# Zero products put into the finished order, and a start in which TensorE transposes the first tiles

## The chip, the cores and the metric

The kernel runs on one core of a Trainium2 chip. The core has five engines that run side by side, each with its own queue of instructions: TensorE (PE in the profile, with PEld for its weight loads), VectorE (DVE), ScalarE (ACT), GpSimd (POOL) and SyncE (SP), which here issues all DMAs. [...] TensorE writes into eight banks of PSUM, each of 128 partitions by 512 numbers of 32 bits; operands lie in SBUF.

The metric is the device time of one execution in microseconds (us), lower is better. The profile comes from one execution on the chip.

## The reference

Four residual layers work on one sequence x of 2048 tokens by 512 features in bf16: attention, a feed-forward block, then both again with the same weights.

```
x = x + attention(layernorm(x), wqkv, wo)      # 32 heads of 16 features, all 2048 keys for each query
x = x + ffn(layernorm(x), w1, b1, w2, b2)      # 512 -> 1376 -> 512, tanh form of gelu
x = x + attention(layernorm(x), wqkv, wo)
x = x + ffn(layernorm(x), w1, b1, w2, b2)

attention: q, k, v = split(y @ wqkv);  p = softmax(q k' / 4);  out = concat(p v) @ wo
ffn:       gelu(y @ w1 + b1) @ w2 + b2
```

The layernorm has no scale or shift. In the softmax one exp is taken for every head, query and key: 32 x 2048 x 2048 of them in each of the two attention layers.

## The kernel before

The text of the kernel is a planner. `Builder` holds generators, one for each piece of work, that hand tasks to `Sched`. `Sched.run` keeps a model of when each engine is free and when each operand is ready (`Prog.op`, `Prog.ready`), and picks again and again the task that can start first, by priority where several can. Each instruction carries a planned duration, written in the code; from them come the order of the instructions on each engine and which of them share work. After the last task, `finalize` puts in the semaphore waits, and the program is issued engine by engine. On the chip only the order and the waits are left; the planned times have no force there.

**Tiling.** Tokens are handled in 16 tiles of 128. A segment is one group of four heads (hg, 8 of them) with one chunk of 512 queries. The first chunk of layer 1 is done in two parts: keys 0 to 511 first, so that scores can start when four token tiles are through, then the other 1536 keys. Layer 3 splits its first chunk in the same way (1536 keys, then 512), and its last 512 queries into two units of 256.

**Scores.** A score tile is 128 keys by 512 queries of one head (L1240, a matmul on 32 rows of the array, four heads side by side). Most tiles go to ScalarE, which takes the exp of two banks at a time at the start, and of three and two in turn once six banks are free ("wide"), into the tile PT (L1225). Other tiles go to DVE: L1317 forms a bit pattern that stands for the exp, in two tiles of a pair, and L1348 makes three shifted copies of the pair; POOL scales values for them (L1101). Which tiles go to DVE is decided while the order is made, in `take_d`, by how late DVE is in the plan. L1409 multiplies the weights with V into one bank, ACCB, on 32 columns of the array per head.

**Other stages.** `job_first_tile` takes token tiles 0 to 3 of layer 1: layernorm (L808 to L821), a transpose by DMA into yT (L968), K, Q and V matmuls (L989), copies to SBUF (L1000, L1012, L1027), sums of squares for a bound on the scores (L941). Queries go to q_scr in DRAM (L1020) and come back transposed as qraw (L1074), from which L1086 makes QT. `job_qkv_tile` does the same for all other tiles (matmuls L876). `job_post` does the output projection, layernorm and the feed-forward block of a chunk, `job_tail` that of the last unit. SP issues the DMAs in the planned order, each in turn.

**Zero products.** `fill_pe` is called by `Sched.run` whenever TensorE would have a gap of more than 0.2 us in the plan. It looks at how busy the array was in the last 3.41 us of the plan, and where that is under 0.62 it puts matmuls with zero weights into the gap (L1150 on four column tiles, L1153 on the whole array). They add nothing to a result; they are part of the plan like other work, so what is planned later starts behind them. In the lines that follow, `need` is how many are wanted and `n` how many are put in.

```
n = int((gap - (PE_SWITCH if P.tiling == "col" else 2 * PE_SWITCH if P.tiling == "row" else PE_SWITCH) + FILL_OVER) / FILL_T)
need = int((FILL_ACT - P.activity(end)) * 3.41 / FILL_T + 0.999)
n = min(n, need, 80)
```

## Time and profile before

| what | value |
|---|---|
| time, median of 6 runs | 1642.71 us (1640.72 to 1645.58) |
| the profiled execution | 1642.72 us, of which the span from first to last instruction is 1640.9 us |
| granted clock of TensorE, mean over the span | 0.996 |
| ACT busy | 1562.0 us, 95% |
| PE busy | 1554.8 us, 95% |
| DVE busy | 1481.2 us, 90% |
| POOL busy | 379.4 us, 23% |
| exps on ScalarE (L1225) | 1304 instructions, 1485.8 us |
| score tiles on DVE (L1317) | 869 instructions, 584.4 us |
| zero products (L1150) | 2928 instructions, 143.0 us |

Busy time is the time in which an engine has at least one instruction in work; matmuls overlap, so their mean durations are longer than the steps between them. A group of instructions is shown as line, engine, operation, what it writes and reads with shapes, count, then busy us and mean ns, then the engine's idle time just before such instructions and who ended most of it. A row of windows gives, for one stretch of the span, its length and the busy time of PE, PEld, DVE, ACT and POOL with counts, then the clock that TensorE was granted, the mean share in which the DMA engines were busy, and GB/s. A row of the order of time gives start, length, engine, line, operation and count, and in brackets the idle time ahead of it with what ended it.

### The profile page before, as it was taken

Reading aid. Unit: us, or ns where it says so; the run is one execution under the profiler, and the core shown is the slowest. Engines: PE = TensorE matmul, PEld = TensorE weight load, DVE = VectorE, ACT = ScalarE, POOL = GpSimd, SP = SyncE. Lnnn points to the kernel's source line nnn. Section 1 sums busy time; section 2 is a strip of 40 time slices with the busy share of each in tenths; the row PEclk is TensorE's granted clock in tenths of the full one; section 3 lists DMA queues with packets and bytes.
Section 4 is the critical chain, followed back from the end, with each engine's and each line's share of the span. In section 5 each row is a group of like instructions: output and inputs, shape, how many; then the busy total and the mean of one; then the engine's idle time right before and its main releaser. Section 6 shows DMA issues by size and latency. Waiting matters only on the chain.

```text
span 1640.9 us, 40475 instructions
## 1 busy us (share of the span) xinstructions
PE 1554.8 (95%) x16682; PEld 504.1 (31%) x16833; DVE 1481.2 (90%) x3255; ACT 1562.0 (95%) x1383; POOL 379.4 (23%) x575
## 2 busy tenths in 40 slices
PE   8989999999999999999999998999999999999998
PEld 4222222222222222222232222322222222344444
DVE  7789999989999899989979799999899989999894
ACT  4989999999999999999999999899999999999996
POOL 4354332111320112111121134511011101222220
PEclk9999999999999999999999999999999999999999
DMA  6572000103111121112291330000000100010000
GB/s 174 103 138 56 21 8 8 43 17 65 63 24 36 32 44 57 33 30 46 86 127 45 64 84 15 18 21 8 14 11 8 21 12 8 6 19 10 23 8 14
DMA packets 181238, 66.34 MB, mean 40 GB/s; under 512 B 160859, under 2 KB 175424, under 8 KB 181056
## 3 DMA queue, kind: packets, MB, share of 16 engines
q1 hardware_dynamic: 181056, 63.75, 17.6%
q8 instruction: 135, 2.21, 0.5%
q14 instruction: 47, 0.39, 0.1%
HBM read 19.96 MB, written 15.30 MB: 21 GB/s over the span
## 4 chain that ended last, share of the span: by engine, by line
PE 48%; DVE 26%; ACT 21%; issue 3%; DMA 1%; POOL 1%; DVEq 0%; SPq 0%
ACT PT L1225 20%; PE ps L1240 19%; PE ps L1409 14%; DVE dp L1317 9%; DVE dp L1348 7%; PE ps L1574 4%; PE ps L1536 4%; PE ps L1503 3%; PE ps L876 3%; PE ps L1150 2%; DVE accT L1439 1%; ACT h L1566 1%; DVE n L941 1%; DVE OT L1479 1%; DVE QT L1086 1%
## 5 line engine op out<-in xcount | busy, mean ns | idle before, releaser
L1225 ACT ACTIVATE PT<-ps 128x1024 bf16<-128x1024 f32 (+1 forms) x1304 | 1485.8, 1251 | 49.1 <-PE ps L1240 42.7
L1240 PE MATMUL ps<-QT,KT 32*128 32x512 bf16 (+1 forms) x4608 | 685.4, 358 | 44.7 <-DVE dp L1317 15.5
L1317 DVE TENSOR_SCALAR dp<-ps 128x512 uint16<-128x512 f32 x869 | 584.4, 680 | 76.2 <-PE ps L1240 72.1
L1348 DVE TENSOR_SCALAR dp<-dp 128x1024 uint16<-128x1024 uint16 (+1 forms) x1323 | 515.7, 431 | 7.0 <-PE ps L1409 1.9
L1409 PE MATMUL ps<-PT,V 128*17 128x512 bf16 (+1 forms) x3624 | 487.8, 359 | 0.5 <-DVE accT L1439 0.4
L1101 POOL TENSOR_SCALAR vs<-V 128x340 bf16<-128x340 bf16 (+3 forms) x240 | 242.8, 1012 | 846.5 <-PE ps L1409 809.2
L1409 PE MATMUL ps<-dp,vs 128*17 128x512 bf16 (+1 forms) x2952 | 434.4, 356 | 1.2 <-DVE dp L1348 0.9
L1240 PEld LDWEIGHTS ps<-QT,KT 32*128 32x128 bf16 x4608 | 178.0, 91 | 575.5 <-issue 152.5
L1409 PE MATMUL ps<-dp,V 128*17 128x512 bf16 (+1 forms) x984 | 208.6, 358 | 1.5 <-DVE accT L1439 0.6
L1409 PEld LDWEIGHTS ps<-PT,V 128*17 128x17 bf16 x3624 | 116.0, 88 | 114.8 <-issue 103.2
L1409 PEld LDWEIGHTS ps<-dp,vs 128*17 128x17 bf16 x2952 | 109.5, 88 | 126.5 <-issue 107.0
L1150 PE MATMUL ps<-wqkv,zw 128*32 128x256 bf16 x2928 | 143.0, 278 | 0.6 <-DVE accT L1439 0.6
L1536 PE MATMUL ps<-yT,wf 128*128 128x512 bf16 (+3 forms) x356 | 93.7, 357 | 6.9 <-issue 4.3
L876 PE MATMUL ps<-wqkv,xnT 128*128 128x512 bf16 x299 | 85.4, 387 | 9.2 <-issue 2.9
L1150 PEld LDWEIGHTS ps<-wqkv,zw 128*32 128x32 bf16 x2928 | 73.4, 96 | 59.0 <-issue 41.8
L1439 DVE STREAM_TRANSPOSE accT<-ps 128x512 f32<-128x512 f32 (+1 forms) x88 | 57.9, 658 | 10.4 <-PE ps L1409 10.2
L1503 PE MATMUL ps<-wo,OT 128*128 128x512 bf16 x209 | 60.8, 382 | 5.0 <-issue 3.7
L1560 DVE TENSOR_SCALAR h<-ps,b1c 128x512 bf16<-128x512 f32 (+2 forms) x88 | 61.8, 702 | 3.9 <-PE ps L1536 3.5
L1409 PEld LDWEIGHTS ps<-dp,V 128*17 128x17 bf16 x984 | 51.1, 88 | 45.5 <-issue 24.9
L1479 DVE STREAM_TRANSPOSE OT<-ob 128x512 bf16<-128x512 bf16 (+1 forms) x72 | 45.9, 638 | 0.2
L1536 PEld LDWEIGHTS ps<-yT,wf 128*128 128x128 bf16 (+1 forms) x396 | 27.7, 99 | 53.1 <-issue 29.7
L1574 PE MATMUL ps<-wf,h 128*128 128x512 bf16 x143 | 40.8, 382 | 3.1 <-issue 1.7
(171 smaller groups left out, 774.6 us busy)
## 6 DMA issues: line engine op xcount, KB each, us to landing
wf<-in_B_w_dram SPq DMA_DIRECT2D x90, 128.0 KB, 2.3
q_scr<-qk SPq DMA_DIRECT2D x22, 256.0 KB, 2.1
k_scr<-qk SPq DMA_DIRECT2D x12, 256.0 KB, 2.0
out_dram<-xres SPq DMA_DIRECT2D x16, 128.0 KB, 1.7
v_scr<-vst SPq DMA_DIRECT2D x12, 136.0 KB, 1.9
V<-v_scr SPq DMA_DIRECT2D x8, 204.0 KB, 4.9
wqkv<-in_A_wqkv_dram SPq DMA_DIRECT2D x3, 512.0 KB, 5.7
q_scr<-h SPq DMA_DIRECT2D x6, 256.0 KB, 2.0
```

Of the source, the lines that this page charges most:

```text
L876: yield Task("pe", prio, [I(lambda e, c=c: e.matmul(self.ps[:, b, :], lhsT=xnT[:, c, :], rhs=self.wqkv[:, c, which * 512:which * 512 + 512 ...
L1101: yield Task("pool", 0.8, [I(lambda e, k=k: e.tensor_scalar(out=self.vs[:, q, k - 1, i:i + n, :], in0=src, scalar1=WSHIFT[k], scalar2=None ...
L1150: P.op("pe", lambda e, p=p: e.matmul(self.ps[p:p + 32, b, 0:w], lhsT=self.zw[:, 0:32], rhs=rhs[:, 0:w], start=st, stop=st, skip_group_chec ...
L1225: S_.submit(Task("act", 1e-5 * gi, [I(lambda e, pt=pt, n=n, b0=b0: e.activation(out=self.PT[:, pt:pt + n, :], in_=self.ps[:, b0:b0 + n, :] ...
L1240: return [I(lambda e, kb=kb, i=i: e.matmul(self.ps[:, b, i * W:(i + 1) * W], lhsT=self.KT[32 * hp:32 * hp + 32, hg, kb * 128:(kb + 1) * 12 ...
L1317: self.S_.submit(Task("dve", 0.0, [I(lambda e: e.tensor_scalar(out=self.dp[:, u, w * 512:(w + 1) * 512], in0=self.ps[:, b, :], scalar1=BIT ...
L1348: yield Task("dve", pr, [I(lambda e, k=k, v=v: e.tensor_scalar(out=self.dp[:, v, 0:N], in0=self.dp[:, u, 0:N], scalar1=float(SHIFT[k]), sc ...
L1409: ops.append((i, I(lambda e, hp=hp, v=v, ap=ap[:, i * W:(i + 1) * W], first=first and i == 0, W=W: e.matmul(self.ps[32 * hp:32 * hp + 17, ...
L1439: yield Task("dve", 0.3, [I(lambda e: e.transpose(self.accT[:, a, 0:W], self.ps[:, ACCB, 0:W]), [("ps", ACCB)], [RA], 0.17 + 0.535 * W / 5 ...
L1503: yield Task("pe", pr, [I(lambda e, hg=hg, i=i, b=b: e.matmul(self.ps[:, b, :], lhsT=self.OT[:, hg, i * 128:(i + 1) * 128], rhs=self.wo[:, ...
L1536: yield Task("pe", pr, [I(lambda e, c=c: e.matmul(self.ps[0:M, b, off:off + W], lhsT=self.w1(fc, c), rhs=self.yT[:, c, 0:W], start=(c == 0 ...
L1574: yield Task("pe", pr, [I(lambda e, fc=fc, i=i, b=b: e.matmul(self.ps[:, b, :], lhsT=self.gt(fc, i, W), rhs=self.w2(L, fc), start=(fc == 0 ...
```

## The change

Line numbers of the diff's new side are not those of the profile.

**Zero products.** `fill_pe` no longer puts any in while the order is made; it still lets DVE take a score tile in a long gap. When the order is finished, `refill` walks through it once more with a fresh model: before each TensorE instruction it computes the gap that the plan leaves, and puts in passes of four zero matmuls of 256 columns as long as the least busy stretch of 3.414 us around that moment holds less than 0.45 of the array. The order of all other instructions stays as it was made. A pass may go to ACCB, to the spare bank, or to a score bank whose contents have been read. Zero matmuls read `zw` alone, now 256 columns wide.

**Start.** All of x for tiles 0 to 3 is loaded ahead of the three weight slices. The other x tiles come in six pieces of two tiles, from a task of their own (`late`): it starts after the K store of tile 3, and the last four pieces wait for the query load of segment 2. Before, there were two pieces of four and eight tiles. `job_first_tile` transposes the normalised tile with four TensorE transposes and a copy by ScalarE in place of the DMA. The constants on DVE that aren't needed at once become tasks of priority 1.9.

**Planned durations and small rules.** DMA durations are set anew, and a DMA with a size also waits for a model of the shared bus; exps go from 0.174 + 0.428 n to 0.19 + 0.4275 n for n banks, the overlap of ScalarE's instructions from 0.127 to 0.128, the shifted copies of L1348 from 0.151 to 0.163 plus the same slope; PV_IDLE, the time after which a small batch of L1409 is let go, from 0.25 to 0.5; the post work of chunk 2 in layer 1 gets priority 0.95 in place of 1.6; batches of L1409 are sorted by turn.

The built programs differ in these counts: exps of three, two and one banks 620, 683, 1 before and 617, 682, 0 after; score tiles on DVE 869 and 881; pairs of shifted copies 1284 and 1305, single ones 39 and 33; zero matmuls of 32 columns of weights 2928 (256 wide) and 136 (128 wide) before, and 3216 (256 wide) after; zero matmuls on the whole array 154 (128 wide) and 36 (256 wide) before, none after; four yT transposes by DMA before, sixteen on TensorE and four copies on ScalarE after.

```diff
@@ Prog.op
         op.t0 = max(self.free[eng], self.ready(eng, reads, writes, same_ok))
         if eng == "sp":
             self.free[eng] = op.t0 + dur
-            op.t1 = op.t0 + dur + (2.0 if lat is None else lat)
+            lat, size = lat if isinstance(lat, tuple) else (2.0 if lat is None else lat, 0.0)
+            op.t1 = max(op.t0 + dur + lat, self.bus + 0.9)
+            if size:
+                self.bus = max(self.bus, op.t1 - size) + size
+                op.t1 = self.bus
@@ build_startup
         ldx(0, 1)
-        ldw(1, 512)
         ldx(1, 2)
         ldx(2, 4)
+        ldw(1, 512)
         ldw(0, 0)
         ldw(2, 1024)
-        self.S_.when([("ks", 1, 1)], lambda: ldx(4, 8))
-        self.S_.when([("ks", 1, 3)], lambda: ldx(8, 16))
+        def late():
+            yield ("keys", [("ks", 1, 3)])
+            for a in range(4, 16, 2):
+                if a == 8:
+                    yield ("keys", [("qraw", 2)])
+                yield self.dma(lambda e, a=a: e.dma_start(self.xres[:, a:a + 2, :], xr[:, a:a + 2, :]), [], [("x", a), ("x", a + 1)], 1.7, 0.5, (2.24, 1.04))
+                self.S_.mark(("xld", a))
+        self.S_.spawn(late(), 1.7)
@@ job_first_tile
-        yield self.dma(lambda e: e.dma_start_transpose(xnT, xnr), [RX], [RXT], prio, 1.25)
+        b = yield ("get", "mb")
+        yield Task("pe", prio - 0.5, [I(lambda e, k=k: e.transpose(self.psbf(b)[:, k * 128:(k + 1) * 128], xnr[:, k * 128:(k + 1) * 128], self.ident[:, :]), ...) for k in range(4)])
+        yield Task("act", prio - 0.5, [I(lambda e: e.activation(out=xnT, in_=self.psbf(b)[:, 0:512].rearrange("p (c t) -> p c t", c=4), func=ACTF.Copy), ...)])
+        S_.release("mb", b)
@@ fill_pe, refill
-        n = min(n, need, 80)
...
+        def need(t):
+            k = int(t / FILL_DT)
+            lo = max(0, k - m + 1)
+            s = sum(act[lo:lo + m])
+            best = s
+            for j in range(lo, min(k, n - m - 1)):
+                s += act[j + m] - act[j]
+                best = min(best, s)
+            return FILL_U * FILL_W - best
...
+            t0, b, st = min(banks)
+            d = FILL_N / 2400.0
+            while t0 + d <= end and need(t0 + d / 2) > 0.0:
+                for p in range(4):
+                    z = self.zero(b, p, FILL_N, st)
+                    P.op("pe", z[0], z[1], z[2], z[3], z[4], z[5])
+                add(t0, t0 + d, 1.0)
+                t0 += d
+        for op in old.ops:
+            if op.eng == "pe":
+                fill(op)
+            P.op(*op.spec)
@@ flow_scores
-                                                [("ps", b) for b in banks], [("pt", pt + k) for k in range(n)], 0.174 + 0.428 * n)]),
+                                                [("ps", b) for b in banks], [("pt", pt + k) for k in range(n)], 0.19 + 0.4275 * n)]),
@@ try_pv
-PV_IDLE = 0.25
+PV_IDLE = 0.5
@@ post_prio
-        return 0.95 if (L, qc) == (1, self.NC - 1) else 1.6 if (L, qc) == (1, self.NC - 2) else 2.2
+        return 0.95 if L == 1 and qc >= self.NC - 2 else 2.2
@@ build
         S_.run()
+        self.refill()
```

## The prediction

> **What bounds it.** I read the page first (busy time, then the costliest groups), next the windows by stage, then the order of time of ScalarE in the first 100 us, then the windows around each fall of the clock.
>
> The page's busy times, and two lines of the groups kept apart by shape (count, busy us, mean ns, idle before them):
> ```profile
> PE 1554.8 (95%) x16682; PEld 504.1 (31%) x16833; DVE 1481.2 (90%) x3255; ACT 1562.0 (95%) x1383; POOL 379.4 (23%) x575
> ...
> L1225 ACT ACTIVATE PT<-ps 128x1536 bf16<-128x1536 f32 x620 | 914.4, 1475 | 32.9 <-PE ps L1240 26.6
> L1225 ACT ACTIVATE PT<-ps 128x1024 bf16<-128x1024 f32 x683 | 711.5, 1049 | 16.3 <-PE ps L1240 16.0
> ```
> TensorE and ScalarE both show 95%, but TensorE's holds 143 us of zero products (L1150) and overlapped matmuls. ScalarE's holds almost nothing but exps. So I count ScalarE's idle time, 78.9 us of 1640.9, by stage (columns: PE, PEld, DVE, ACT, POOL busy, clock, DMA):
> ```profile
> 26.00:94.00 68.00, 63.45 (x521) 20.03 (x524) 50.24 (x106) 60.04 (x64) 20.54 (x33) 0.95 0.54 110
> 94.00:170.00 76.00, 67.89 (x661) 19.95 (x656) 72.36 (x163) 70.24 (x65) 40.41 (x93) 0.98 0.45 98
> 170.00:750.00 580.00, 555.88 (x5467) 157.83 (x5518) 539.53 (x1165) 571.15 (x494) 112.19 (x145) 1.00 0.14 33
> 750.00:1000.00 250.00, 239.69 (x2403) 72.47 (x2424) 225.47 (x496) 240.08 (x206) 52.79 (x103) 1.00 0.37 75
> 1000.00:1050.00 50.00, 42.61 (x565) 15.52 (x561) 47.53 (x102) 41.54 (x44) 29.61 (x48) 0.97 0.09 20
> 1050.00:1620.00 570.00, 546.71 (x6778) 192.90 (x6825) 520.84 (x1160) 562.24 (x485) 104.74 (x101) 1.00 0.06 13
> ```
> Idle: about 16 us before 26, then 8.0, 5.8, 8.9, 9.9, 8.5, 7.8, and 14 in the tail. From 170 to 750 ScalarE is 98.5% busy: there only fewer or shorter exps help. The start and the layer change have something to give back.
>
> ScalarE at the start, in order of time:
> ```profile
> 26.23 7.44 ACT L1225 ACTIVATE PT<-ps 128x1024 bf16<-128x1024 f32 x8 [2.75 <-PE ps L1240]
> 35.58 1.02 ACT L1225 ACTIVATE PT<-ps 128x1024 bf16<-128x1024 f32 x1 [1.92 <-PE ps L1240]
> 37.09 1.02 ACT L1225 ACTIVATE PT<-ps 128x1024 bf16<-128x1024 f32 x1 [0.48 <-PE ps L1240]
> 38.58 1.02 ACT L1225 ACTIVATE PT<-ps 128x1024 bf16<-128x1024 f32 x1 [0.47 <-PE ps L1240]
> 40.94 1.02 ACT L1225 ACTIVATE PT<-ps 128x1024 bf16<-128x1024 f32 x1 [1.34 <-PE ps L1240]
> ```
> First exp at 26.23; after eight (one segment) it starves, since the second segment's queries come late: the last q_scr store (SP, 25.0) shares the DMA engines with the 1 MB x load issued at 23.03 and lands 6.9 us later; the transposed reload L1074 takes 2.6 more. Then the clock falls:
> ```profile
> 31.86:35.27 3.41, 1.25 (x18) 0.44 (x14) 2.61 (x9) 1.81 (x2) 0.86 (x1) 1.00 0.34 76
> 35.27:38.69 3.42, 3.24 (x26) 0.93 (x26) 3.22 (x11) 2.16 (x3) 1.22 (x2) 0.50 0.41 87
> 38.69:42.10 3.41, 3.25 (x9) 0.64 (x8) 1.90 (x6) 1.94 (x2) 0.13 (x1) 0.50 0.52 105
> 120.61:124.02 3.41, 3.08 (x20) 0.39 (x16) 2.01 (x6) 2.49 (x3) 0.83 (x1) 0.50 0.85 174
> 1018.31:1021.73 3.42, 3.42 (x49) 1.50 (x47) 2.40 (x7) 2.54 (x3) 0.00 (x0) 0.50 0.02 5
> ```
> These are all the falls: 6.8, 3.4 and 3.4 us. Adding the matmul rows of the trace by columns (0.215 us per 512, the step between two and four L876 in the chain; a quarter for a 32-row or 32-column tile), the stretches just before them held 0.14, 0.31 and 0.25 of a full array; the lowest that had no fall held 0.33.
>
> [...] the q_scr stores at the start land in 4.0 to 6.7 us, against a median of 2.0 to 2.1 over the run. [...]
>
> **The change, part by part.**
> *Start.* Before: DVE builds constants until 6.32, the first statistics end 7.50, the power on POOL lets L821 start at 9.02, four DMA transposes (1.26 each on SP, 2.5 to landing) follow, the first matmul starts at 12.29, the first K copy at 13.14, the first exp 13.1 us later. After, by the built order: DVE takes the first statistics ahead of ten of the constants, as x tile 0 lands (issue 0.72 plus 3.2 = 3.9). Statistics 0.65, V memset 0.48 and aggregate 0.2 give 5.2; POOL has rs 0.2, a memset pair of 1.3 queued ahead of the power, and the power 0.6: 7.3. Apply 0.4, four transposes 0.4 (bounds 0.2 to 0.9), ScalarE's copy 0.6 (like L1012, 0.58), four matmuls and handovers 1.0: K copy at 9.8, 3.3 earlier. K's weights now stand behind all of x, 1 MB in all: at the 252 GB/s of 5 to 10 us some 4.2 us after about 2.5, so 6.7, ahead of need at 8.7. Those constants (4.05 to 6.32 now) hide in DVE's idle time, 7 us of the first 25.7; without that cover they cost their 2.3. The four yT copies cost nothing, ScalarE being idle. Bounds 0 to -5; I take -3.2.
>
> *x in 256 KB pieces, last eight tiles after the third query load.* The 1 MB load leaves the q_scr stores' way. With two pieces still beside them I take landing 3.5 us after the last issue: reload 2.6, QT 0.4, score and handover 0.5, so 7.0 after that issue, about 6 after the first exp starts; eight exps last 7.3. The starving goes, and the first fall with it. What is late next: QKV of tiles 4 to 15. By scores, the built order puts 18 to 20 L876 into each of five stretches of 16 scores (before: 10 to 20). In the order of time, eight narrow exps with 16 to 18 L876 between them take 8.4 to 8.6 us (46.30 to 54.89 to 63.30), without any 7.3. So 7.3 + 7.3 + 5 x 8.5 + 7.7 = 64.8 us for 64 exps, against 96.50 - 26.23 = 70.3 now: -5.5. Bounds: -11 (all at 7.3) and -1 (five at 9.3, the slowest eight with no starving, 87.18 to 96.50).
>
> *Exps.* The planner's duration of an exp rises; in the plan three banks cost 1.345 and two 0.917, where back-to-back exps start 1.331 and 0.904 apart in the trace. It moves twelve more score tiles to DVE: exps 620/683/1 (three, two, one bank) become 617/682/0, so 3 x 1.331 + 0.904 + 0.48 = -5.4 us on ScalarE. DVE gets 12 loads x 0.680 and 21 - 6 shifts (0.435, 0.30): +15.5 us in 160 of idle; TensorE 36 PV matmuls, four abreast, +1.9.
>
> *Zero products.* In passes of 256 columns over the whole array, 862 become 804 (0.107 to 0.115 us each by the steps between x8, x16 and x20): 6 us less TensorE, worth 0 where ScalarE bounds. They are put in once the order stands, so they no longer shape it, towards 0.45 of the array in every 3.414 us against 0.62 of the past window. 0.45 is 0.12 above the lowest that held. I take the falls at 120 and 1018 as gone: ScalarE idled 0.9 + 0.6 in and after the first, 0.9 in the second: -2.4.
>
> *Rest.* PV_IDLE, post_prio and DMA durations re-deal the order: no row prices it; 750 to 1050 holds 18.4 us of idle, so -6 to +6, taken 0. The last exp has two banks, not one: +0.4. DVE, 95% busy in 94 to 170, takes x work later: +2.
>
> Sum: -3.2 - 5.5 - 5.4 - 2.4 + 0.4 + 2.0 = -14.1. The profiled execution took 1642.72 us (span 1640.9 and 1.8 around it), the median is 1642.71: 1628.6.
>
> **Rivals.**
> *Zero products ahead of scores (slower).* A pass is emitted where the plan has a gap. If TensorE runs behind the plan, it stands in front of a ready score and costs ScalarE 0.107. The 804 are 86 us; the gain is gone from 132 on, one in six. At one in four: 201 x 0.107 = 21.5, so 1650. For it: in 26 to 94 TensorE paces ScalarE, and exps wait 42.7 us for scores in all. Against it: 862 such passes now leave 98.5% in the long stage.
> *DVE becomes the bound.* It is 93% busy in 170 to 750 and gets 15.5 us. Then the 5.4 is lost and the start's 8.7 stays: 1634. For it: scores wait for DVE's loads already (L1240 behind dp L1317, 15.5 and 69.9 us at the weight load). Against: 160 us of idle.
> *It doesn't do what it says.* Clock falls stay (1 to 1.5 us each), and the re-dealt layer change gives the start back: about 1641.
>
> **Chances.** Mine 0.55 (own range 1621 to 1637), DVE 0.22, no gain 0.09, slower by zero products 0.14. About 0.2%, 3.3 us, is what a measurement can tell. Faster 0.78, same 0.08, slower 0.14. The range, 1617 to 1646, takes in the lower bound of the start and the re-dealing, and leaves out most of the slower case.
>
> **What would show it.** First exp near 23; no gap after the eighth; exp 64 ends near 88, not 96; exps 617 and 682 with the same means; clock without 3.4 us stretches at 0.5; ACT about 1559 busy. Wrong, if exps wait more for L1240 than 42.7 us with zero products just before, if DVE's waits at L1317 vanish while ScalarE idles, or if 750 to 1050 idles more than 18.4 us.

## The result: slower by 0.7%

The changed kernel takes 1656.92 us (median of 36 runs, 1644.73 to 1667.67), the kernel before 1643.32 in the same comparison (73 runs). The ratio is 1.0072 with a 95% interval of 1.0059 to 1.0084. I had forecast 1628.6. Ratios are taken over all the runs and not between two medians; two runs of one later kernel (target 0.8), more than 1.5% above its fastest, are left out of its ratio. The profiled execution took 1657.36 us, with a span of 1655.6 at a mean granted clock of 0.982; before it was 1640.9 at 0.996.

The page's busy times and the granted clock in 40 slices, of the kernel after:

```profile
PE 1562.4 (94%) x16703; PEld 486.1 (29%) x16847; DVE 1493.1 (90%) x3282; ACT 1558.4 (94%) x1382; POOL 379.9 (23%) x575
...
PEclk9989999999999999999899997999999999999999
```

The exps in the groups kept apart by shape (count, busy us, mean ns, idle before them):

```profile
L1281 ACT ACTIVATE PT<-ps 128x1536 bf16<-128x1536 f32 x617 | 912.0, 1478 | 38.0 <-PE ps L1296 32.3
L1281 ACT ACTIVATE PT<-ps 128x1024 bf16<-128x1024 f32 x682 | 712.8, 1052 | 33.3 <-PE ps L1296 32.4
```

ScalarE has the 617 and 682 exps of the forecast and is 3.5 us less busy than before. But it waits 64.7 us for scores (L1296) where it waited 42.6. The windows by stage (columns: PE, PEld, DVE, ACT, POOL busy, clock, DMA):

```profile
26.00:94.00 68.00, 60.97 (x489) 18.49 (x493) 49.09 (x106) 56.01 (x59) 23.86 (x36) 0.93 0.71 117
94.00:170.00 76.00, 69.95 (x686) 20.17 (x694) 72.44 (x166) 70.00 (x65) 35.80 (x84) 0.95 0.32 81
170.00:750.00 580.00, 552.19 (x5415) 152.57 (x5461) 537.59 (x1164) 566.13 (x491) 114.23 (x153) 1.00 0.14 37
750.00:1000.00 250.00, 236.55 (x2244) 67.48 (x2260) 225.12 (x486) 229.35 (x197) 48.64 (x93) 0.95 0.33 68
1000.00:1050.00 50.00, 48.21 (x517) 13.36 (x515) 44.48 (x102) 43.78 (x44) 23.12 (x42) 0.87 0.09 17
1050.00:1620.00 570.00, 541.91 (x6686) 184.98 (x6736) 531.46 (x1176) 558.76 (x482) 115.52 (x115) 1.00 0.06 13
```

ScalarE's idle time by stage, against before: 11.9 (16.3) ahead of 26, then 12.0 (8.0), 6.0 (5.8), 13.9 (8.9), 26.9 (18.4) from 750 to 1050, 11.2 (7.8), and about 15 (14) in the tail. That is 18 us more, less the 3.5 of busy time: the 14.7 by which the span grew. The largest piece is the stretch from 750 to 1050, where layer 3 begins: the one that I had left at nothing.

The clock column is the other half. Before, three falls of the clock to 0.5 made 13.7 us. Now there are six: at 40.3 (6.8 us), 91.5 (10.2), 794.6 (10.2), 862.9 (3.4), 989.2 (23.9) and 1617.2 (3.4), together 58.0 (falls behind the last exp's work, at the very end, are left out here and below). Over the 36 runs the time and the mean clock lie on a line (correlation -0.98): 12.0 us for each 0.01 of clock. On that line the kernel after takes 1642.1 at the 0.996 of before, and 1637.3 at a full clock; 51 runs of the kernel before give 1638.4 at a full clock. So at an equal clock the change is worth about -1 us, and the whole loss goes with the clock. That is a relation, not yet a cause.

### How one fall looks

Windows cut at the clock's own edges, at the switch to layer 3's second part:

```profile
985.77:989.18 3.41, 1.97 (x24) 0.49 (x23) 2.43 (x9) 3.41 (x4) 3.04 (x6) 1.00 0.37 113
989.18:992.60 3.42, 3.34 (x31) 0.90 (x31) 2.86 (x9) 1.92 (x3) 3.16 (x5) 0.50 0.60 172
992.60:996.01 3.41, 3.41 (x31) 0.82 (x31) 2.10 (x5) 2.07 (x2) 0.75 (x2) 0.50 0.36 56
996.01:999.42 3.41, 3.41 (x31) 0.71 (x28) 1.93 (x5) 2.00 (x3) 0.00 (x0) 0.50 0.00 0
...
1009.66:1013.08 3.42, 3.42 (x24) 0.77 (x22) 1.97 (x7) 2.28 (x2) 0.00 (x0) 0.50 0.17 38
1013.08:1016.49 3.41, 3.37 (x51) 1.16 (x47) 3.32 (x9) 2.70 (x4) 1.74 (x3) 1.00 0.01 2
```

In the first window ScalarE is fully busy (3.41) but TensorE only 1.97; by columns that is 0.29 of a full array. Then the clock is at 0.50 for seven windows, 23.9 us. TensorE is busy for 3.34 to 3.42 us of each of them, and ScalarE gets scores for only 1.8 to 2.5 us.

All engines in order of time in that first window:

```profile
986.43 0.39 PE L1296 MATMUL ps<-QT,KT 32*128 32x512 bf16 x3 [0.21 <-ACT PT L1281]
...
986.66 0.27 DVE L1075 TENSOR_REDUCE kmx<-ps 32x1 f32<-32x128 bf16 x1
986.67 1.34 POOL L973 TENSOR_SCALAR qt<-qt 128x32 f32<-128x32 f32 x1
...
987.34 0.60 PE L1296 MATMUL ps<-QT,KT 32*128 32x512 bf16 x3
...
988.30 0.57 POOL L1077 TENSOR_TENSOR kmx<-kmx,chalf 32x1 f32<-32x1 f32 x1
...
988.90 0.30 DVE L1078 TENSOR_SCALAR krhs<-mask,kmx 32x8 bf16<-32x8 f32 x1 [0.98 <-POOL kmx L1077]
...
989.26 0.18 PE L1080 MATMUL ps<-krhs,sel 32*128 32x8 bf16 x1 [1.31 <-DVE krhs L1078]
```

These are the scale factors that the next part's queries need (`job_scl`): maximum on DVE, power on POOL, product on DVE, a small matmul L1080. The power stands behind the bound rows of a token tile (L973, 1.34 us) in POOL's queue, DVE waits 0.98 for the power, and L1080 waits 1.31 at the head of TensorE's queue. TensorE does nothing else in that time. In the kernel before the last step of the same chain started at 976.7 (here at 990.0), and no fall follows before 1018.

By columns, the seven windows at half clock held 0.33, 0.33, 0.32, 0.27, 0.26, 0.29 and 0.34 of a full array: within the 0.12 to 0.37 of the windows ahead of the falls of all runs here. What ends a fall is not shown: the seventh window, after which the clock came back, held about as much as the first.

### The profile page after: what moved, and what is told of

It reads as the page before. It is cut to its first block, busy times and chain, and to the rows that moved or that the text cites. A ratio compares the mean times of both kernels' runs of the same rounds, so it can differ in the third digit from the quotient of the medians.

```text
span 1655.6 us, 39668 instructions
## 1 busy us (share of the span) xinstructions
PE 1562.4 (94%) x16703; PEld 486.1 (29%) x16847; DVE 1493.1 (90%) x3282; ACT 1558.4 (94%) x1382; POOL 379.9 (23%) x575
## 4 chain that ended last, share of the span: by engine, by line
PE 39%; DVE 31%; ACT 23%; issue 2%; DMA 2%; POOL 1%; SPq 0%; POOLq 0%; DVEq 0%
ACT PT L1281 22%; PE ps L1296 14%; PE ps L1470 11%; DVE dp L1373 11%; DVE dp L1404 8%; PE ps L1635 4%; PE ps L1597 3%; PE ps L895 3%; PE ps L1564 2%; DVE accT L1500 1%; DVE OT L1540 1%; PE ps L1209 1%; DVE st L825 1%; DMA xnT<-xn 1%; DVE QT L1111 1%
## 5 line engine op out<-in xcount | busy, mean ns | idle before, releaser
L1281 ACT ACTIVATE PT<-ps 128x1024 bf16<-128x1024 f32 (+1 forms) x1299 | 1479.9, 1255 | 71.2 <-PE ps L1296 64.7
L1296 PE MATMUL ps<-QT,KT 32*128 32x512 bf16 (+1 forms) x4608 | 685.4, 362 | 37.5 <-ACT PT L1281 14.9
L1373 DVE TENSOR_SCALAR dp<-ps 128x512 uint16<-128x512 f32 x881 | 592.3, 680 | 69.9 <-PE ps L1296 67.4
L1404 DVE TENSOR_SCALAR dp<-dp 128x1024 uint16<-128x1024 uint16 x1338 | 522.7, 432 | 11.4 <-PE ps L1470 6.8
L1470 PE MATMUL ps<-PT,V 128*17 128x512 bf16 (+1 forms) x3612 | 473.2, 363 | 0.0
L1296 PEld LDWEIGHTS ps<-QT,KT 32*128 32x128 bf16 x4608 | 169.3, 91 | 578.1 <-ACT PT L1281 276.5
L1209 PE MATMUL ps<-zw 128*32 128x256 bf16 x3216 | 148.1, 284 | 2.6 <-DVE ps L704 1.6
L1470 PEld LDWEIGHTS ps<-PT,V 128*17 128x17 bf16 x3612 | 111.7, 88 | 112.0 <-issue 98.1
L895 PE MATMUL ps<-wqkv,xnT 128*128 128x512 bf16 x301 | 89.8, 399 | 13.4 <-issue 3.7
L1209 PEld LDWEIGHTS ps<-zw 128*32 128x32 bf16 x3216 | 77.0, 98 | 68.3 <-issue 42.2
L1470 PEld LDWEIGHTS ps<-dp,V 128*17 128x17 bf16 x996 | 48.8, 88 | 56.7 <-issue 26.9
L833 POOL TENSOR_SCALAR rs<-mv 128x4 f32<-128x4 f32 (+2 forms) x19 | 4.6, 245 | 176.8 <-DVE mv L826 176.6
```

Of the source, the lines that this page charges most:

```text
L895: yield Task("pe", prio, [I(lambda e, c=c: e.matmul(self.ps[:, b, :], lhsT=xnT[:, c, :], rhs=self.wqkv[:, c, which * 512:which * 512 + 512 ...
L1209: return I(lambda e: e.matmul(self.ps[32 * p:32 * p + 32, b, 0:w], lhsT=self.zw[:, 0:32], rhs=self.zw[:, 0:w], start=st, stop=st, skip_gro ...
L1281: S_.submit(Task("act", 1e-5 * gi, [I(lambda e, pt=pt, n=n, b0=b0: e.activation(out=self.PT[:, pt:pt + n, :], in_=self.ps[:, b0:b0 + n, :] ...
L1296: return [I(lambda e, kb=kb, i=i: e.matmul(self.ps[:, b, i * W:(i + 1) * W], lhsT=self.KT[32 * hp:32 * hp + 32, hg, kb * 128:(kb + 1) * 12 ...
L1373: self.S_.submit(Task("dve", 0.0, [I(lambda e: e.tensor_scalar(out=self.dp[:, u, w * 512:(w + 1) * 512], in0=self.ps[:, b, :], scalar1=BIT ...
L1404: yield Task("dve", pr, [I(lambda e, k=k, v=v: e.tensor_scalar(out=self.dp[:, v, 0:N], in0=self.dp[:, u, 0:N], scalar1=float(SHIFT[k]), sc ...
```

## The experiments

Each kernel was timed in turn with the kernel before on the same chip; the ratio is to those runs, so ratios compare across groups. The parts of the change are called **start** (x in pieces, constants as tasks, first tiles transposed by TensorE), **durations** (all planned times), **rules** (PV_IDLE, post_prio, order of the PV matmuls, `same_ok` of scores) and **second walk** (`refill`).

### 1. Too few zero products?

My first theory was that 0.45 is too low a target. Two kernels raise it (`FILL_U = 0.62` and `0.8`; 992 and 1008 passes of 256 columns in place of 804), one puts the old `fill_pe` back into the kernel after (1023 passes), and one gives the second walk alone to the kernel before (709).

```diff
-FILL_U = 0.45
+FILL_U = 0.62          # the other: 0.8
```

```diff
-        self.refill()   # after with the old filler: fill_pe, activity and zw of before in its place
```

```diff
         S_.run()
+        self.refill()   # before with the second walk: fill_pe keeps only its solo score tiles
```

> The changed kernel with the target of the second walk at 0.62 of the array in place of 0.45, so 992 passes of zero products in place of 804; all other instructions in the same order. Theory (too few passes, so that the clock falls where the chip runs behind the plan): mean clock back to 0.993 or more, time 1641 to 1646 us. Rival (the re-dealt order itself is slower, and the clock falls follow from its stalls): clock stays near 0.983 and time near 1657. Rival (passes stand ahead of scores): time above 1657, with a higher clock.

> The changed kernel with the target at 0.8: 1008 passes, nearly every planned gap that can hold one; order of all else the same. Theory: like 0.62 or better by 0 to 3 us, since only 16 passes more find a gap: 1639 to 1645, clock 0.993 or more. Rival (order): 1657. Rival (passes ahead of scores): slower than with 0.62.

> The changed kernel's start, durations and rules, but with zero products put in while the order is made, as before (0.62 of the past window, 1023 passes); no second walk. Theory (the second walk at 0.45 is the loss, the rest a small gain): 1636 to 1643, clock 0.994 or more. Rival (order and durations are the loss): 1650 or more.

> The kernel before, with only the zero products changed: the second walk at 0.45, 709 passes in place of 862; start, durations and rules as before (the order differs in part, since passes no longer shape it: 876 score tiles on DVE). Theory: the clock falls, mean 0.98 to 0.987, and time rises by 10 to 16 us to 1653 to 1659. Rival (order and durations of the change are the loss): clock 0.995, time 1641 to 1645.

| kernel | median, us (runs) | ratio, 95% interval | median clock |
|---|---|---|---|
| after, target 0.62 | 1657.68 (22) | 1.0065, 1.0049 to 1.0081 | 0.984 |
| after, target 0.8 | 1658.83 (14) | 1.0059, 1.0030 to 1.0087 | 0.985 |
| after, old `fill_pe` | 1664.06 (6) | 1.0112, 1.0083 to 1.0141 | 0.976 |
| before, second walk alone | 1645.39 (22) | 1.0006, 0.9992 to 1.0020 | 0.995 |

The theory fell. A quarter more zero products changes neither time nor clock, and with the two higher targets the falls of 24 and 31 us at 990 and 987 are still there. A pass can go only where the plan has a gap, and the wait at L1080 is not in the plan. The second walk alone costs the kernel before nothing that these runs can tell (interval 0.9992 to 1.0020). So the loss is in the order that start, durations and rules produce.

### 2. Which part of the change?

Each of the three was taken back alone in the kernel after, and the start put alone into the kernel before. The core of "durations back":

```diff
-OVERLAP = {"act": 0.128, "dve": 0.08, "pool": 0.05}
+OVERLAP = {"act": 0.127, "dve": 0.08, "pool": 0.05}
-  [("pt", pt + k) for k in range(n)], 0.19 + 0.4275 * n)]),
+  [("pt", pt + k) for k in range(n)], 0.174 + 0.428 * n)]),
-  ... dma_start_transpose(xnT, xnr), [RX], [RXT], prio, 1.31, 1.2)
+  ... dma_start_transpose(xnT, xnr), [RX], [RXT], prio, 1.25)
```

and so on for every planned time in the diff. "Start back" has

```diff
-        ldx(0, 1); ldx(1, 2); ldx(2, 4); ldw(1, 512)
+        ldx(0, 1); ldw(1, 512); ldx(1, 2); ldx(2, 4)
...
-        self.S_.spawn(late(), 1.7)
+        self.S_.when([("ks", 1, 1)], lambda: ldx(4, 8))
+        self.S_.when([("ks", 1, 3)], lambda: ldx(8, 16))
...
-        yield Task("pe", prio - 0.5, [I(lambda e, k=k: e.transpose(...
+        yield self.dma(lambda e: e.dma_start_transpose(xnT, xnr), ...
```

with the constants in one go; the same lines the other way round are the new start in the kernel before. "Rules back":

```diff
-PV_IDLE = 0.5
+PV_IDLE = 0.25
-        return 0.95 if L == 1 and qc >= self.NC - 2 else 2.2
+        return 0.95 if (L, qc) == (1, self.NC - 1) else 1.6 if (L, qc) == (1, self.NC - 2) else 2.2
-                    ops.append((nth[j, sh] + 0.1 * i, ...
+                    ops.append((i, ...
-  [("ps", b)], W / 2400.0, [("ps", b)], ("row", hp)) for i, kb in enumerate(kbs)]
+  [("ps", b)], W / 2400.0, [("ps", b)] if i else [], ("row", hp)) for i, kb in enumerate(kbs)]
```

> The kernel after, with the planner's durations as before (exps 0.174 + 0.428 n, shifts 0.151, DMA issues and landings, no shared bus); start, rules and second walk of the zero products stay. The output is the reference's. Theory 'durations': the new durations re-deal the order so that the chain of the scale factors is just in time at the switches of part and layer, and TensorE stalls there; so this one comes back to 1643 (ratio 0.998 to 1.002, mean clock 0.995). Theory 'start' or theory 'rules': it stays at 1652 to 1660, clock 0.98. Theory 'any re-deal loses': 1650 to 1660 as well.

> The kernel after, with the start as before: K's weights after the first x tile, x in two large loads, constants in one go on VectorE, first four tiles transposed by DMA; new durations, rules and second walk stay. The output is the reference's. Theory 'start': x in pieces makes the later tiles late, TensorE starves at 40 and at 88 us and what follows is thrown out of its plan; so this one gives 1643 to 1648 with a first exp near 26, and the falls of the clock after 90 us go too. Theory 'durations' or 'rules': first exp near 26, about 3 us more than the kernel after at the start, falls at the switch of layer (980 to 995 us) stay, 1655 to 1662.

> The kernel after, with the four rules as before: idle limit of the PV batches 0.25, priority 1.6 for the last but one chunk of layer 1, PV matmuls sorted by their place in the pick, repeated score writes without the exemption; start, durations and second walk stay. The output is the reference's. Theory 'rules': more PV batches wait for 0.5 us of idle TensorE and layer 1's last post-processing stands ahead of what the switch of layer needs; so this one comes back to 1640 to 1645, clock 0.995. Theory 'durations' or 'start': 1652 to 1660, clock 0.98, falls at the switch of layer stay.

> The kernel before with the new start alone (x tiles first, six later x loads in pieces, constants as tasks, first four tiles transposed by TensorE); durations, rules and zero products inside the walk as before. The output is the reference's. If the start is worth what I put in the sum (3.2 for the first exp, 5.5 for the x pieces): 1634 to 1638. If the x pieces only move the starving from the ninth exp to the eighteenth, as the trace of the kernel after shows: 1640 to 1643. Theory 'start' as the cause of the loss: 1650 to 1656 with a lower clock. Theory 'any re-deal loses': 1650 or more, whatever the first exp does.

| kernel | median, us (runs) | ratio, 95% interval | median clock |
|---|---|---|---|
| after, old durations | 1636.30 (6) | 0.9945, 0.9927 to 0.9962 | 0.997 |
| after, old start | 1656.47 (7) | 1.0084, 1.0053 to 1.0115 | 0.990 |
| after, old rules | 1657.39 (6) | 1.0073, 1.0055 to 1.0091 | 0.994 |
| before, new start alone | 1665.01 (6) | 1.0121, 1.0094 to 1.0148 | 0.987 |

In the kernel after it is the durations. Without them the change makes the kernel 0.55% faster, some 9 of the 14 us that I had forecast; this version beats both kernels. Its windows by stage:

```profile
26.00:94.00 68.00, 63.45 (x561) 19.55 (x563) 51.03 (x106) 60.63 (x64) 20.20 (x33) 0.97 0.59 115
94.00:170.00 76.00, 71.31 (x779) 21.39 (x769) 73.61 (x168) 71.63 (x67) 41.41 (x93) 1.00 0.46 99
170.00:750.00 580.00, 563.42 (x5473) 153.51 (x5467) 538.07 (x1173) 569.80 (x495) 112.35 (x147) 1.00 0.15 36
750.00:1000.00 250.00, 240.91 (x2367) 68.96 (x2366) 232.51 (x511) 242.57 (x211) 57.99 (x109) 1.00 0.32 67
1000.00:1050.00 50.00, 45.68 (x615) 15.61 (x612) 47.34 (x107) 45.91 (x46) 28.41 (x46) 1.00 0.09 20
```

From 750 to 1050 ScalarE idles 11.5 us, against 26.9 in the kernel after; the scale factors are done at 975.8, not at 990.0; and the clock falls once, for 3.4 us at 40.7, while exps remain.

The two kernels with old start and old rules show that the clock is not all. Their median clock came back in part, to 0.990 and 0.994, and their time did not. On the lines over their own few runs they take about 1646 and 1651 us at a full clock, where the kernel after takes 1637. They are slow for another reason. The start alone lost 20 us, which of my expectations only the one for any re-deal allowed; section 4 comes back to it.

### 3. Which durations, and is it only luck?

The exp, shift and overlap times were taken back alone, then all the others (called the DMA side: issue and landing times, the shared bus, and the small ones of the start). As a test of luck, the kernel with all old durations got an overlap of 0.128 in place of 0.127, 1 ns less for every planned exp. The new durations were also put alone into the kernel before. The edit for the exp:

```diff
-  [("pt", pt + k) for k in range(n)], 0.19 + 0.4275 * n)]),
+  [("pt", pt + k) for k in range(n)], 0.174 + 0.428 * n)]),
-  self.dres(v), 0.163 + 0.2605e-3 * N)])
+  self.dres(v), 0.151 + 0.2605e-3 * N)])
```

with the overlap at 0.127; the DMA side is the rest of the diff in section 2, and the test of luck is

```diff
-OVERLAP = {"act": 0.127, "dve": 0.08, "pool": 0.05}
+OVERLAP = {"act": 0.128, "dve": 0.08, "pool": 0.05}
```

> The kernel after, with only the planner's exp and shift as before (0.174 + 0.428 n, overlap 0.127, shift 0.151), so that three banks cost 1.331 and two 0.903 in the plan, which is what back-to-back exps take in the trace; the DMA durations stay new. The output is the reference's. Theory 'exp': the longer planned exp gives VectorE some 20 score banks more than the kernel with all old durations and makes the plan run later than the chip, so it loses time everywhere; this one comes to 1636 to 1640, clock 0.995 or more. Theory 'DMA': it stays at 1650 to 1660, clock 0.98 to 0.985. Theory 'any re-deal': anything from 1636 to 1660, with no relation to which part was taken back.

> The kernel after, with only the DMA side of the planner as before (issue and landing times, no shared bus, engines free at 0, the start's small durations); exps 0.19 + 0.4275 n, overlap 0.128 and shift 0.163 stay new. The output is the reference's. Theory 'DMA': the plan's new landing times order the loads and what waits for them so that TensorE's queue head meets a DMA or the scale chain at 88 and 988 us; this one comes to 1636 to 1641 with the falls at 88 to 93 and 987 to 990 gone. Theory 'exp': it stays at 1650 to 1660. Theory 'any re-deal': anything from 1636 to 1660.

> The kernel after with all durations as before (the one that gave 1636.3), but the planned overlap of ScalarE at 0.128 in place of 0.127: every exp is planned 1 ns shorter, and nothing else is touched. The output is the reference's. If the old durations are what makes the order good: 1634 to 1640, as a nanosecond can't matter to that. If any re-deal can lose or win some us through the stalls and the clock that it happens to meet: a time at least 5 us away from 1636.3, most likely in 1642 to 1660.

> The kernel before with the planner's new durations alone (exps, shifts, DMA issues and landings with a shared bus, engines free from 0.75); start, rules and zero products inside the walk as before. The output is the reference's. Theory 'durations': it loses what the change loses and more, 1650 to 1660 with a clock of 0.98 to 0.985. Theory that the durations are bad only together with the new start or rules: 1640 to 1646. Theory 'any re-deal': 1640 to 1660.

| kernel | median, us (runs) | ratio, 95% interval | median clock |
|---|---|---|---|
| after, old exp, shift and overlap | 1646.48 (14) | 1.0019, 1.0000 to 1.0037 | 0.988 |
| after, old DMA side | 1647.69 (21) | 1.0023, 1.0009 to 1.0036 | 0.994 |
| after, all old, overlap 0.128 | 1636.03 (5) | 0.9948, 0.9934 to 0.9963 | 0.991 |
| before, new durations alone | 1662.35 (4) | 1.0107, 1.0090 to 1.0124 | 0.988 |

All durations together are worth 1.27% (1.0072 to 0.9945). Each half alone gives back about 0.5%. Neither of my two theories had this: both halves count. Put alone into the kernel before, the durations cost 1.07%. The nanosecond changed the order (layer 3's first scale factors at 772.7 in place of 791.3, and the falls lie elsewhere), but not the time (its median clock is lower, 0.991 against 0.997, so at an equal clock it would be the faster order).

That one new order kept its time doesn't make the old durations better in themselves. Four pairs of kernels differ in the durations alone:

| the rest of the kernel | ratio with old durations | ratio with new durations |
|---|---|---|
| kernel before | 1 | 1.0107 |
| rules and second walk, old start | 0.9990 | 1.0084 |
| start, rules and second walk | 0.9945 | 1.0072 |
| start and second walk, old rules | 1.0122 | 1.0073 |

In three of them the new durations cost about 1%; in the fourth they gain 0.5%, and the intervals (1.0095 to 1.0149, 1.0055 to 1.0091) don't overlap. (0.9990 and 1.0122 are measured in section 4.) So the new durations cost in most of these orders but not in all, which points to what each order meets on the chip.

The trace of the kernel before with new durations shows one such thing. Its first exp starts at 35.56, 9.3 us later than before:

```profile
31.87 0.69 DVE L813 BATCH_NORM_STATS2 st<-xres 128x6 f32<-128x512 bf16 x1 [6.07 <-DMA xres<-in_A_x_dram]
...
32.74 0.18 PE L1061 MATMUL ps<-krhs,sel 32*128 32x8 bf16 x1 [6.87 <-DVE krhs L1059]
...
35.56 1.02 ACT L1230 ACTIVATE PT<-ps 128x1024 bf16<-128x1024 f32 x1 [10.51 <-PE ps L1245]
```

In the new order the statistics of a later x tile (L813) stand ahead of the product of the scale chain (L1059) in VectorE's queue. The power that L1059 needs was done at 25.7, but VectorE waits 6.07 us for the x load first. The sixty-fifth exp still starts 8.9 us later than in the kernel before (105.4 against 96.5). That is about half of the 18.7 us that the durations cost there, and it begins as a wait for a load, not with the clock, which falls inside that wait (at 28.0, for 10.2 us).

Why the new exp, shift and overlap times are worse here is argued, not shown. Back-to-back exps start 1.331 and 0.904 us apart in the trace; the old plan has 1.331 and 0.903, the new one 1.345 and 0.917. Over 1299 exps the new plan is 17 us longer than what the chip needs. Within the DMA side no single entry was tried.

The kernel with the old exp time also corrects a step of my working. Its groups by shape:

```profile
L1281 ACT ACTIVATE PT<-ps 128x1536 bf16<-128x1536 f32 x617 | 916.9, 1486 | 32.6 <-PE ps L1296 26.8 <-PE ps L1080 0.4
L1281 ACT ACTIVATE PT<-ps 128x1024 bf16<-128x1024 f32 x682 | 718.7, 1061 | 28.7 <-PE ps L1296 28.3
```

617 and 682 exps, as after, though the planned exp is the old one; with the new exp time and the old DMA side they are 620 and 683, as before. So the twelve tiles went to VectorE with the DMA side, not with the exp's planned duration.

### 4. Is it the wait or the fall, and what are the other parts worth?

To tell the wait from the fall, 12 zero passes were put ahead of L1080 at the two switches of layer 3, gap or not. The order of all other work is unchanged.

```diff
             if op.eng == "pe":
                 fill(op)
+                if ("krhs",) in op.spec[2]:
+                    chain += 1
+                    if chain > 2:
+                        for i in range(12):
+                            for p in range(4):
+                                z = self.zero(op.spec[3][0][1], p, FILL_N, True)
+                                P.op("pe", z[0], z[1], z[2], z[3], z[4], z[5])
             P.op(*op.spec)
```

> The kernel after, with 12 more zero passes ahead of the scale chain's second matmul (krhs x sel) at each of the two switches in layer 3, whether the plan has a gap there or not; the order of all other instructions is the same. The output is the reference's. Theory 'the fall costs': the 1.3 us of wait at 988 are filled, the window before holds over 0.5 of the array, the 23.9 us of half clock after it go, in which ScalarE lost 8.9 us, and the 10.2 us at 794 go with some 3: 1643 to 1648, clock 0.990. Theory 'the wait costs': the falls go, but the stall and the passes stay: 1654 to 1660. Theory 'falls are drawn at random': they move elsewhere, 1654 to 1660 at a clock of 0.98 to 0.985.

Measured: 1644.80 us (14 runs), ratio 0.9998, 0.9983 to 1.0012, median clock 0.993. That is 12 us less than the kernel after, for 24 passes put in (the second walk then found room for 47 fewer elsewhere, so there are 781 in all, where after has 804). TensorE in order of time at this switch:

```profile
987.80 0.60 PE L1304 MATMUL ps<-QT,KT 32*128 32x512 bf16 x3
988.34 1.49 PE L1217 MATMUL ps<-zw 128*32 128x256 bf16 x48
990.00 0.16 PE L1080 MATMUL ps<-krhs,sel 32*128 32x8 bf16 x1 [0.17 <-DVE dp L1412]
990.00 0.39 PE L1304 MATMUL ps<-QT,KT 32*128 32x512 bf16 x3
```

The windows at the edges used above:

```profile
985.77:989.18 3.41, 3.21 (x58) 1.35 (x62) 2.62 (x9) 3.41 (x4) 2.59 (x5) 1.00 0.48 151
989.18:992.60 3.42, 3.13 (x50) 1.08 (x43) 3.23 (x10) 2.99 (x3) 3.22 (x6) 1.00 0.48 144
992.60:996.01 3.41, 3.41 (x49) 1.04 (x45) 3.41 (x8) 3.31 (x4) 1.41 (x3) 1.00 0.36 84
996.01:999.42 3.41, 3.14 (x33) 0.74 (x27) 3.41 (x8) 3.40 (x4) 1.20 (x2) 1.00 0.00 0
```

The chain is no earlier: L1080 and the next scores start at 990.00 (in the kernel after at 989.26 and 990.35). But the first window now holds 0.52 of an array in place of 0.29, no fall follows, and over the nine windows to 1016.5 ScalarE is busy 29.9 us where it was 21.1. The wait cost next to nothing; the fall behind it cost 8.7 us in 23.9, or 0.37 us for each us at half clock. That agrees with the line over the runs: 0.01 of mean clock is 33 us at half clock, and 12.0 / 33 is 0.36. The gain arises at this place: the 751st exp starts at 952.3 in the kernel after and at 952.8 here, the 801st at 1021.0 and at 1011.8. The fall at 794 is gone as well, and one of 6.8 us stands at 678 that the kernel after doesn't have.

In the same group, the kernel with old durations lost the rules, the start, or got a target of 0.62.

The edits are those of section 2: rules back, start back, and `FILL_U = 0.62`.

> The kernel with all old durations that gave 1636.3, without the four rules: so before, with the new start and the second walk. The output is the reference's. The start alone on the kernel before gave 1665. If the rules make the gain and heal the start: 1655 to 1665. If the second walk heals it, and the start is worth what I put down for it: 1634 to 1638. If each order is its own case: between.

> The kernel with all old durations that gave 1636.3, without the new start: so before, with the four rules and the second walk. The output is the reference's. If the gain of 8 us comes from the start, as in my sum (8.7): 1643 to 1647. If it comes from the rules: 1634 to 1638. If each order is its own case: up to 1660.

> The kernel with all old durations that gave 1636.3, with the target of the second walk at 0.62 in place of 0.45; the order of all else is the same. The output is the reference's. The clock is at 0.997 there, so at some 11 us for 0.01 there are 3 us to be had at most: 1633 to 1636. If the further passes stand in front of ready scores: 1637 to 1642.

| kernel, all with old durations | median, us (runs) | ratio, 95% interval | median clock |
|---|---|---|---|
| start and second walk, no rules | 1663.93 (6) | 1.0122, 1.0095 to 1.0149 | 0.987 |
| rules and second walk, no start | 1642.84 (14) | 0.9990, 0.9974 to 1.0006 | 0.998 |
| all three, target 0.62 | 1636.80 (8) | 0.9946, 0.9928 to 0.9963 | 0.997 |

With the rules (and old durations) the start is worth 0.45%, some 7 us. Without them it loses 1.2%, with or without the second walk. The rules without the start are worth 0.16% (0.9990 against 1.0006), which the intervals don't tell from nothing. More zero products do nothing where there are no such waits.

The trace of the start alone shows where it loses. ScalarE at the switch into layer 3:

```profile
822.22 2.37 ACT L1244 ACTIVATE PT<-ps 128x1536 bf16<-128x1536 f32 x2 [0.18 <-PE ps L1259]
834.30 10.69 ACT L1244 ACTIVATE PT<-ps 128x1536 bf16<-128x1536 f32 x9 [9.72 <-PE ps L1259]
852.03 8.21 ACT L1244 ACTIVATE PT<-ps 128x1024 bf16<-128x1024 f32 x7 [7.04 <-PE ps L1259]
```

It waits 9.72 us until layer 3's first scale factors are there (L1074 at 832.34), and 7.04 us more while TensorE does output projections of layer 1 (L1522) ahead of the next scores. The clock was full in both waits. The kernel with start and second walk has the same two, of 10.26 and 6.52 us; from 750 to 850 ScalarE idles 15.5 us with the start alone and 3.8 in the kernel before. Up to this switch the start alone was not behind: its 661st exp starts at 817.3, in the kernel before at 820.0.

### 5. Which rule, and does the cure carry over?

One rule was put back alone: the priority of layer 1's last but one chunk, 1.6 for 0.95. And the 12 passes went into the order with the overlap of 0.128, where L1076 (the same small matmul) waits 0.85 us and a fall of 10.2 us follows at 772.

```diff
-        return 0.95 if L == 1 and qc >= self.NC - 2 else 2.2
+        return 0.95 if (L, qc) == (1, self.NC - 1) else 1.6 if (L, qc) == (1, self.NC - 2) else 2.2
```

> The kernel with all old durations (1636.3), with the priority of layer 1's last but one chunk back at 1.6 from 0.95; start, the other three rules and the second walk stay. The output is the reference's. If it is this priority that the new start needs: 1655 to 1665, and layer 3's first scale factors come after 660 exps or more, near 830 us. If it is the idle limit of the PV batches or their order: 1634 to 1640.

> The kernel with all old durations and the planned overlap of ScalarE at 0.128 (1636.0, clock 0.991), with 12 zero passes ahead of the scale chain's second matmul at each of the two switches in layer 3; the order of all else is the same. The output is the reference's. Theory 'the fall costs, and waits of 0.9 us and more set it off': the fall of 10.2 us at 772 goes, in which ScalarE lost some 2.3 us of its 10.2, and the clock rises by 0.003: 1631 to 1634. If the 12 passes of 1.3 us are as dear as the wait of 0.85: 1636 to 1639.

The priority gave 1645.77 us (14 runs), ratio 1.0005, 0.9987 to 1.0023: a third of the 27 us that all four rules make, and between the two ranges that I had expected. So it is one of the things that the start needs, not the only one. Layer 3's first scale factors come after 668 exps, at 831.7 us, as expected (639 and 791.3 with the new priority). The stretch from 750 to 850 in this kernel, and then in the one with the new priority:

```profile
750.00:850.00 100.00, 92.71 (x986) 29.67 (x993) 78.47 (x166) 83.88 (x73) 9.41 (x26) 1.00 0.41 86
```

```profile
750.00:850.00 100.00, 96.03 (x968) 26.67 (x969) 94.43 (x207) 96.25 (x85) 19.21 (x33) 1.00 0.42 80
```

ScalarE idles 16.1 us there, against 3.7, at a full clock. It is again the two waits of the start alone, here 8.54 and 6.52 us: with the old priority, the loss at this switch is back, and it is not the clock's.

The passes in the other order missed: 1640.08 us (18 runs), ratio 0.9965, 0.9948 to 0.9983, no gain on 1636.03 (5 runs). The fall at 772 is gone from the profiled execution, but the median clock is 0.991 as without them, and falls of 10.2 us stand at 1022 and 1401 instead. So the cure worked at a wait with a long fall behind it, as at 989; here it is not shown to help.

## Why the prediction was wrong

- **What bounds the kernel, and counting ScalarE's idle time by stage:** right. Idle and busy time of ScalarE account for the 14.7 us of the span.
- **Exps, -5.4:** 617 and 682 as forecast, busy time 1558.4 (forecast 1559). The counts came from the built program; the cause given for them was wrong: the DMA side of the durations moves the tiles. What the planned exp, shift and overlap do in the kernel after, and I had nothing for, is 0.5% of the time.
- **Start, -3.2:** the first exp starts at 23.78, 2.4 earlier, near the 23 that I gave. Four transposes by TensorE (L988) take 0.40 us there and ScalarE's copy 0.60, as in the sum. But that first exp is one execution's: with the higher targets (0.62 and 0.8), the same start began at 24.9 and 26.9. With the old DMA side it began at 26.3 to 27.0, no earlier than before. ScalarE's idle time up to 94 us is 23.9 in the kernel after and 21.0 with old durations, so the earlier first exp was given back within 70 us.
- **x pieces, -5.5:** half right. ScalarE in order of time at the start:

```profile
23.78 15.91 ACT L1281 ACTIVATE PT<-ps 128x1024 bf16<-128x1024 f32 x17 [1.93 <-PE ps L1296]
41.54 1.02 ACT L1281 ACTIVATE PT<-ps 128x1024 bf16<-128x1024 f32 x1 [1.86 <-PE ps L1296]
43.58 1.02 ACT L1281 ACTIVATE PT<-ps 128x1024 bf16<-128x1024 f32 x1 [1.02 <-PE ps L1296]
...
94.53 1.02 ACT L1281 ACTIVATE PT<-ps 128x1024 bf16<-128x1024 f32 x1 [2.89 <-PE ps L1296]
```

The starving after the eighth exp is gone, as I said, and the first four q_scr stores land in 2.4 to 3.9 us, where before they took 4.0 to 6.7. The starving stands after the seventeenth now, and a second one comes at 91.6. TensorE in order of time there:

```profile
90.03 0.40 PE L1296 MATMUL ps<-QT,KT 32*128 32x512 bf16 x2
92.47 1.48 PE L895 MATMUL ps<-wqkv,xnT 128*128 128x512 bf16 x3 [2.04 <-DVE xn L838]
```

A QKV matmul heads the queue 2 us before its operands are there; the window before the fall at 91.5 held 0.16 of an array. I asked what is late next and answered with the number of QKV matmuls, as if each were ready when its turn came. So 64 exps took 77.1 us, from the first to the start of the sixty-fifth, against 64.8 forecast and 70.3 before. Seventeen of these us ran at half clock; at 0.37 they make 6. The same start in other orders came near the forecast: 65.8 us in the kernel before, and 65.1 with all old durations and the overlap of 0.128, but 70.2 with all old durations. So the step can hold, and the order decides whether it does.
- **Zero products, -2.4 (the falls at 120 and 1018 taken as gone):** this step failed. "0.45 is 0.12 above the lowest that held" compared a share of the plan with shares on the chip. The window at 985.8 held 0.29 on the chip, since a wait that the plan lacks can't be filled by a walk over the plan's gaps. Falls grew from 13.7 to 58.0 us, worth some 16 us at 0.36 (an estimate from the two rates above).
- **Rest, "taken 0":** this step failed most. "No row prices it" was true, but the range of -6 to +6 was worked from ScalarE's idle time in one stage, as if a new order could only add or remove waits there. The forecast's own sign of being wrong came true: 26.9 us of idle from 750 to 1050, against 18.4. Durations alone cost the kernel before 1.07%, half of it at the start; and the rules decide whether the start gains 7 us or loses 20.
- **Rivals.** "Zero products ahead of scores (slower)" named a time near the result, 1650, for a cause that isn't there: 188 further passes changed nothing. VectorE as the bound: it has 160 us of idle time before and after. "Clock falls stay" was the nearest in kind, at 1 to 1.5 us each; the fall at 989 alone cost 8.7.

What stays open: which planned DMA time does its half; why the planned exp, shift and overlap cost; why the new durations gain where the rules are old; which of the other rules gives the remaining two thirds; and where the kernels with old start and with old rules lose what they lose at a full clock.

## What to carry to other kernels

In a kernel whose order is made from planned durations, a change of these is a change of the whole order: try it alone, and measure it, even where every new number looks closer to the chip. Zero products that are to keep a clock up can miss a wait that the plan doesn't have: read the array's share in the window before each fall, find the instruction at the head of TensorE's queue, and try the passes there. It gave 12 us in one kernel here and nothing in another; to have the operands there earlier was not tried. And where a part gains only beside another (the start here, beside the rules), neither can be judged by itself.

## What the runs showed that I had not expected

- A fall of the clock can last much longer than what set it off: after 1.3 us of wait, seven windows of 3.41 us, and in another kernel (the old `fill_pe` in the kernel after) ten, 34.1 us at 235.7, though TensorE was busy for 3.34 to 3.42 us of each of the seven.
- Its price is nearly linear over the runs of these two kernels: 9.8 to 13.4 us for 0.01 of mean clock in the groups of the kernel before, 12.0 for the kernel after. It isn't fixed: with the old priority of section 5, a run at a clock of 0.945 took 1655.6 us, only 9.8 above the median at 0.995.
- These traces show no sharp share below which the clock falls. By columns, the windows ahead of all 80 falls in the twenty profiled executions held 0.12 to 0.37 of an array; at a full clock one of 0.27 went by without a fall (996.9, the old `fill_pe` in the kernel after), and one of 0.28 (1001.4, old durations without the start). In the trace of the kernel after, L895 has 301 matmul records for 336 weight loads; if those are missing records, single shares are a little low.
- One load that comes late can hold up work that doesn't need it: in the kernel before with new durations, VectorE waited 6.07 us for x with the scale chain behind it, and the first exp came 9.3 us later.
